# The last layers' first product: two side-by-side 64-row matmuls become two full 128-row ones

## The chip, the cores and the metric

The kernel runs on one NeuronCore of a Trainium2 chip. The metric is device time in microseconds (us) of one execution, as the median of several runs. Beside the times there is one profiled execution of each kernel, from which all rows below come. TensorE multiplies matrices from SBUF into PSUM banks, VectorE, ScalarE and GpSimd do elementwise work, and SyncE issues the DMAs.

## The reference, cut to what matters

A recurrence over 768 steps for 4 batches of 8 heads gives 3072 tokens of 320 values. Two pairs of layers follow. The change lies in the last pair, `_moe2_ref`:

```python
x = _moe_ref(x=x, **moe_kwargs)            # 3072 x 320
h = x @ w_in                               # w_in: 320 x 2048
g = np.maximum(h, 0.0) + alpha * np.minimum(h, 0.0)
return (g @ w_out).astype(np.float32)      # w_out: 2048 x 320
```

## The kernel before

The recurrence runs in 24 slots of chunks (phase 1). Between its products stand those of the first pair of layers. Phase 2 does the rest: the first pair's last tokens, and the whole second pair.

Numbers are float32 held as two parts, a high one that TensorE takes as it is and a low one, the rest. A product of x and w is done as high times high, high times low and low times high. In the second pair the first product contracts 320 inputs, as two row tiles of 128 and one of 64, transposed so that inputs lie on the rows and tokens in the columns. `x2_d[w]` in DRAM holds a window of 256 tokens as five tiles: the high and low part of rows 0 to 127, those of rows 128 to 255, and a fifth tile with the high part of the last 64 inputs in rows 0 to 63 and their low part in rows 64 to 127. The weights' third row tile holds its 64 inputs twice (`_layout` stacks `n[256:]` on itself), so one 128-row matmul with the high weights (`wh[2]` by `x[4]`) covers high times high and high times low for the last inputs. What is left of them is the low weights by the high inputs.

The hidden units are 16 tiles of 128 (`K2`). `mm3` does the first product for one or two of them into PSUM tiles `ph`; the moving rows are the tokens, 256 or 512 columns. Seven matmuls of 128 rows each (line 1016), then one of 64 rows (line 1019). For the first tile of a pair that last one uses rows 0 to 63 of the low weights and of `x[4]`; for the second it uses rows 64 to 127 of the weights and a sixth tile `x[5]`, into which `load_x` (line 1005) loads the high part once more at rows 64 to 127. The two therefore stand in different halves of the array. Then VectorE applies the slope in two steps (`leaky`, lines 595 and 596), ScalarE makes the high part `gh` (line 1025) and GpSimd the low part `gll` (line 1026).

`mm4` does the second product: for each 128 tokens three matmuls of 320 columns into an accumulator `acc` (lines 1037 to 1039). `step` calls `mm3` for the new tiles and then `mm4` for tiles that are older by `LAG`, 2: while VectorE, ScalarE and GpSimd work on a pair, TensorE does the second product of the pair before.

The windows come in groups. The first, `G0`, is window 0 alone, 256 columns, one hidden tile at a time; its 16 steps are threaded by the string `TAIL` between the first pair's last tokens: "s" is a step of `G0`, "a" a first product of the first pair (line 575), "n" its scaling by ScalarE (line 592), "t" and "u" its transposes (line 614), "b" its second product, "o" the transposes out, "w" a load of weights. Then five groups of two windows (512 columns) and one of one window (256 columns) take two tiles a step. The order of TensorE's instructions is the order in which the code is written; the other engines' orders come from a scheduler.

Of the kernel before, what the change touches and what calls it, by code (L numbers as in the profile page):

```python
# [48 lines left out]
def tile_kernel(ctx: ExitStack, tc: tile.TileContext, w_fm, a0_fm, a_fm, kb_fm, r_fm, v_fm, v_tm,  # L49
# [59 lines left out]
    KBP = [ca.tile([128, 1280], F32, name=f"KBS{i}") for i in range(3)]  # L109
    KBS = [t.rearrange("p (e s d) -> p e s d", e=2, d=D) for t in KBP]  # odd heads before even ones  # L110
    XP = ca.tile([128, 320], F32, name="XP")
# [46 lines left out]

# [1 line left out]
    queue, now, seen = [], [0.0], []  # L160
# [28 lines left out]
    def pace(dt, n):  # L189
        """follows dt us in which the array counts n columns: keeps those of the last SPAN us above the floor"""  # L190
        note(dt, n)
        floor, extra = LEVELS[min(st["slot"] // 4, 1) if st["slot"] != 4 else 2] if st["slot"] < NG - 4 else LEVELS[3]
        if more() and counted(dt + 0.09) + n < floor:
            note(0.09, 0)
            while more() and counted() < floor + extra:
                pop()

    def idle(dt):
        """dt us in which the next products wait for other engines"""
        while dt > 0.1 and more():  # L200
            dt -= pop()
        note(max(dt, 0.0), 0)
# [4 lines left out]

# [1 line left out]
    def keep(n):  # L209
# [6 lines left out]

# [1 line left out]
    def prep_load(w):  # L218
# [23 lines left out]
    def check(w, pe):  # L242
        """counts what is out of range"""
        if pe == 0:
            st[w]["H"] = b4.tile([104, 16, 65], F32, name="H")
        wv = st[w]["wt"][pe][:, 0:520].rearrange("p (s k) -> p s k", k=65)[:, :, 1:65]
        for i, sc in ((0, 1.0), (1, -1.0)):
            j = 4 * w + 2 * pe + i
            o = (m1.tile([104, 8, 64], F32, name="over", tag="raw2") if w < 2 else
                 st[w]["H"][:, pe * 8:pe * 8 + 8, 1:65])  # L250
            nc.scalar.activation(out=o, in_=wv, func=AF.Relu, scale=sc, bias=lims[:, i:i + 1],
                                 accum_out=flags[:, j:j + 1])
# [88 lines left out]

# [1 line left out]
    def inverse(W):  # L343
# [62 lines left out]

# [1 line left out]
    def load_g(g):  # L408
# [40 lines left out]
    def blank(p):  # L449
        """zeros in the rows between those of the two heads"""  # L450
        nc.tensor.matmul(p[32:64].rearrange("p s t -> p (s t)"), lhsT=D1[:, 1:17].bitcast(BF16),
                         rhs=D1[:, 0:16 * p.shape[1]].bitcast(BF16), start=True, stop=True)
        note(0.02, 100)
# [96 lines left out]

# [1 line left out]
    def x_move(w):  # L552
# [9 lines left out]

# [1 line left out]
    def mm1(t, piece):  # L564
# [85 lines left out]

# [1 line left out]
    def decode(raw, e, m, o, scales=()):  # L652
        """scales: of column ranges, a factor for each row"""
        v = raw.rearrange("p (n two) -> p n two", two=2)
        low, high = v[:, :, 0], v[:, :, 1].bitcast(I32)
        nc.vector.tensor_scalar(out=e, in0=high, scalar1=0x7FF00000, scalar2=None, op0=ALU.bitwise_and)
        nc.vector.tensor_scalar(out=m, in0=high, scalar1=0xFFFFF, scalar2=None, op0=ALU.bitwise_and)
        nc.scalar.activation(out=e, in_=e, func=AF.Relu, scale=8.0, bias=ebias[0:e.shape[0]])
        nc.scalar.activation(out=f32(m), in_=m, func=AF.Copy, scale=2.0 ** -20, bias=1.0)
        nc.vector.scalar_tensor_tensor(out=e, in0=high, scalar=-0x80000000, in1=e, op0=ALU.bitwise_and,  # L660
                                       op1=ALU.bitwise_or)
        nc.vector.scalar_tensor_tensor(out=f32(m), in0=low, scalar=2.0 ** -52, in1=f32(m), op0=ALU.mult, op1=ALU.add)
        for a, z, sc in scales:
            nc.vector.tensor_scalar(out=f32(m[:, a:z]), in0=f32(m[:, a:z]), scalar1=sc, scalar2=None, op0=ALU.mult)
        nc.gpsimd.tensor_tensor(out=o, in0=f32(m), in1=f32(e), op=ALU.mult)

# [1 line left out]
    def words(src, scales=()):  # L668
        """words of 256 columns a row, or of 512 while the layers' tiles are free, decoded"""
        n = src.shape[1] * src.shape[2]  # L670
        if n > 256:
            st["wide"] = i = 1 - st.get("wide", 0)
            raw = m1.tile([128, 1024], U32, name="raw", tag=("lnh", "P")[i])[:, 0:2 * n]
            em = m1.tile([128, 2, 512], I32, name="wem", tag="lnl")[:, :, 0:n]
            o = raw[:, 0:n].bitcast(F32)
        else:
            raw = m1.tile([128, 512], U32, name="raw2")
            em = m1.tile([128, 2, 256], I32, name="em2")
            o = m1.tile([128, 256], F32, name="dec")
        nc.sync.dma_start(out=raw.rearrange("p (k n) -> p k n", k=src.shape[1]), in_=src.bitcast(U32))  # L680
        decode(raw, em[:, 0], em[:, 1], o, scales)
        return o
# [26 lines left out]
    def cuts(n, wide):  # L709
        """column ranges of 512 or 256"""  # L710
        return [(i, min(i + 512, n)) for i in range(0, n, 512)] if wide else [(i, i + 256) for i in range(0, n, 256)]

# [1 line left out]
    def w2_tasks():  # L714
# [10 lines left out]

# [1 line left out]
    def vec_tasks(w):  # L727
# [25 lines left out]
    def fill_tasks(g):  # L753
        """of the chunk's slot: products that later windows need, by their places in it, and what they wait for"""
        W, c4 = divmod(g, 4)
# [67 lines left out]
    def tail_tasks(g):  # L823
        """of the tokens after the last chunk: transposes in, first products, second ones, transposes out"""
        t1, t2 = g - 3, g - 4
# [128 lines left out]

# [1 line left out]
    KI, KO = 768, 2 * DM  # L956
# [13 lines left out]
    def early_w():  # L970
        """the first weights, where the chunks' preparation was"""
        k = [b2.tile([128, KI + 2 * KO], F32R, name="kbf") for _ in range(2)]
# [9 lines left out]
    def phase2(p2):  # L982
# [12 lines left out]
        def parts(f):  # L995
            """of the weights of 128 hidden units: the three row tiles in, and the rows out"""
            j, q = divmod(f, 2)
            return [([a[:, k * 256 + q * 128:k * 256 + q * 128 + 128] for k in range(3)], b[:, q * DM:q * DM + DM])
                    for a, b in st["w2", j]]

        def load_x(ws, t):
            for i, w in enumerate(ws):
                c = slice(i * 256, i * 256 + 256)
                nc.sync.dma_start(out=f32(t[:, 0:5, c]), in_=f32(x2_d[w][:]))
                nc.sync.dma_start(out=f32(t[64:128, 5, c]), in_=f32(x2_d[w][0:64, 4]))
            return {"x": [t[:, i, 0:256 * len(ws)] for i in range(6)], "n": 256 * len(ws), "ws": ws, "g": {}}

        def mm3(G, fs, sp):
            x, n = G["x"], G["n"]
            ph = [ps_p[i % len(ps_p)].tile([128, 512], F32, name="ph")[:, 0:n] for i in range(len(fs))]  # L1010
            for p, f in zip(ph, fs):
                (wh, _), (wl, _) = parts(f)
                ops = [(wh[0], x[0]), (wh[0], x[1]), (wl[0], x[0]), (wh[1], x[2]), (wh[1], x[3]),
                       (wl[1], x[2]), (wh[2], x[4])]
                for j, (l, r) in enumerate(ops):
                    nc.tensor.matmul(p, lhsT=l, rhs=r, start=j == 0, stop=False)  # L1016
            for i, (p, f) in enumerate(zip(ph, fs)):
                r = slice(64 * i, 64 * i + 64)
                nc.tensor.matmul(p, lhsT=parts(f)[1][0][2][r], rhs=x[4 + i][r], start=False, stop=True)  # L1019
            for p, f in zip(ph, fs):  # L1020
# [28 lines left out]
        def limits():  # L1049
            """whether a decay is out of range"""  # L1050
            nc.vector.tensor_reduce(out=s1, in_=flags, axis=mybir.AxisListType.X, op=ALU.add)
# [13 lines left out]
        def x_tile(i):  # L1065
            return cm.tile([128, 6, 512], F32R, name=("w1h", "w1l")[i % 2])

# [38 lines left out]

# [1 line left out]
    def slow(gs, ps_w):  # L1108
# [244 lines left out]
```

## Time and profile before

| | |
|---|---|
| median of 3 runs | 1180.27 us (1178.73 to 1182.65) |
| span of the profiled execution | 1174.9 us |
| time of the profiled execution around its span | not on the page; the median lies 5.4 us above the span |
| TensorE busy | 994.3 us, 85% of the span |
| VectorE, ScalarE, GpSimd busy | 68%, 44%, 43% |
| mean granted clock of TensorE | 0.896 |

The span goes from the first to the last instruction. Each row of the section on rows is one answer of the trace: a sum over a stretch, a piece of the chain of work that ended last (followed back from the last instruction, so that each piece begins where what it waited for ended), or a line of the timeline with start, duration and what stands on the engine. In the timeline xN merges N instructions of one kind that follow each other, and a duration reaches from the first start to the last end; consecutive matmuls overlap, so starts tell the pace better than durations. The columns after a matmul are the rows and columns of its weights and the shape of its moving rows. Stretches of phase 2 are told by their times: the first group lies between 769.7 and 834.8 us, the five groups of 512 columns between 834.8 and about 1130.6, the last group behind them.

### The profile page before, as it was taken

The numbers are of one execution on the slowest core, as the hardware profiler recorded it, in microseconds if no ns is written. First come the engines' busy times: TensorE is split into PE (matmuls) and PEld (weight loads), VectorE is DVE, ScalarE is ACT, GpSimd is POOL, SyncE is SP. The second block draws the span as 40 slices with busy tenths as digits, with TensorE's granted clock in tenths as the row PEclk, the third lists the DMA queues.
The fourth block names the chain that finished last, engine by engine and source line by source line (L and its number), as shares of the span: only waits on it lengthen the run. The fifth ranks groups of instructions, "written<-read, shape, count | busy, mean of one in ns | idle before, by whom it ended". The sixth has DMA issues, their size and how long they took to land.

```text
span 1174.9 us, 37092 instructions
## 1 busy us (share of the span) xinstructions
PE 994.3 (85%) x15913; PEld 802.3 (68%) x15934; DVE 794.3 (68%) x1610; ACT 516.9 (44%) x1198; POOL 503.1 (43%) x546
## 2 busy tenths in 40 slices
PE   6275686588878978797779878999999999999997
PEld 3233454467666767676667666788888888888886
DVE  8899689978988798879878966556333333333332
ACT  3324454476547663666465647655212121212121
POOL 6848565444434433443444326245233333333332
PEclk8676877789888987888889889999999999999999
DMA  5513344434333433343334333445202020201000
GB/s 167 140 43 94 82 145 123 105 108 126 86 93 107 125 78 93 107 125 78 96 89 119 106 90 94 119 144 169 55 1 73 1 73 1 72 1 48 1 23 15
DMA packets 105423, 100.24 MB, mean 85 GB/s; under 512 B 38244, under 2 KB 84644, under 8 KB 105252
## 3 DMA queue, kind: packets, MB, share of 16 engines
q1 hardware_dynamic: 105252, 97.80, 30.1%
q8 instruction: 127, 2.08, 0.8%
q14 instruction: 44, 0.36, 0.1%
HBM read 72.34 MB, written 25.43 MB: 83 GB/s over the span
## 4 chain that ended last, share of the span: by engine, by line
PE 44%; DVE 32%; ACT 6%; issue 6%; POOL 5%; DMA 5%; SPq 0%; POOLq 0%; DVEq 0%; ACTq 0%
PE ph L1016 13%; PE acc L1037 5%; DVE tmp L354 5%; PE acc L1039 5%; PE acc L1038 5%; DVE LMN L358 4%; PE h L575 4%; DMA kbf<-in_kb_fm_dram 3%; DVE VUS L482 2%; DVE KBS L508 2%; PE ph L1019 2%; DVE XS L336 2%; DVE H L277 2%; DVE P L582 1%; PE pf L465 1%
## 5 line engine op out<-in xcount | busy, mean ns | idle before, releaser
L1026 POOL TENSOR_TENSOR gll<-gt,gh 128x512 fp32r<-128x512 f32 (+1 forms) x112 | 127.1, 1153 | 239.0 <-ACT gh L1025 219.8
L595 DVE TENSOR_SCALAR gt<-ph,al 128x512 f32<-128x512 f32 (+1 forms) x112 | 71.1, 670 | 219.5 <-PE ph L1019 218.0
L1025 ACT CAST gh<-gt 128x512 fp32r<-128x512 f32 (+1 forms) x112 | 61.1, 560 | 268.9 <-DVE gt L596 268.6
L575 PE MATMUL h<-w1h,xt 128*128 128x512 f32 x240 | 104.4, 483 | 16.3 <-ACT h L584 16.3
L312 POOL TENSOR_TENSOR XS<-XS,H 40x512 f32<-40x512 f32 (+1 forms) x48 | 64.9, 1356 | 89.6 <-DVE H L277 53.7
L354 DVE TENSOR_TENSOR tmp<-LMN,LMN 128x87 f32<-128x87 f32 (+25 forms) x189 | 93.5, 506 | 3.4
L1037 PE MATMUL acc<-w2h,gh 128*128 128x320 f32 x288 | 94.0, 326 | 0.0
L1039 PE MATMUL acc<-w2h,gll 128*128 128x320 f32 x288 | 89.1, 309 | 0.3 <-POOL gll L1026 0.3
L1038 PE MATMUL acc<-w2l,gh 128*128 128x320 f32 x288 | 88.9, 309 | 0.0
L211 PE MATMUL busy<-busy 128*128 128x512 bf16 x200 | 61.8, 463 | 28.1 <-DVE tmp L354 22.9
L528 POOL TENSOR_TENSOR YS<-YS,mask 64x512 f32<-64x512 f32 x48 | 64.3, 1339 | 47.6 <-ACT YS L527 42.9
L358 DVE TENSOR_TENSOR LMN<-LMN,tmp 128x87 f32<-128x87 f32 (+25 forms) x189 | 77.1, 419 | 2.7
L575 PEld LDWEIGHTS h<-w1h,xt 128*128 128x128 f32 x240 | 50.0, 219 | 25.8 <-ACT h L584 18.5
L575 PE MATMUL h<-w1l,xt 128*128 128x512 f32 x144 | 67.5, 469 | 0.0
L628 PE MATMUL po<-wo1h,lnh 128*128 128x320 f32 x192 | 66.7, 348 | 0.5 <-DVE lnl L620 0.5
L596 DVE SCALAR_TENSOR_TENSOR gt<-ph,gt 128x512 f32<-128x512 f32 (+1 forms) x112 | 63.9, 606 | 0.5
L630 PE MATMUL po<-wo1h,lnl 128*128 128x320 f32 x192 | 61.5, 320 | 0.2 <-DVE lnl L620 0.2
L629 PE MATMUL po<-wo1l,lnh 128*128 128x320 f32 x192 | 61.5, 320 | 0.0
L211 PEld LDWEIGHTS <-busy 128*128 128x128 bf16 x221 | 23.2, 114 | 55.0 <-DVE busy L945 22.6
L1037 PEld LDWEIGHTS acc<-w2h,gh 128*128 128x128 f32 x288 | 54.1, 188 | 9.6 <-issue 7.4
L581 ACT ACTIVATE P<-h,sm 128x1024 f32<-128x1024 f32 x24 | 26.7, 1114 | 69.0 <-DVE sm L580 65.8
L1016 PE MATMUL ph<-w1h,w2h 128*128 128x512 f32 x180 | 56.6, 396 | 0.0
(214 smaller groups left out, 2718.9 us busy)
## 6 DMA issues: line engine op xcount, KB each, us to landing
kbf<-in_kb_fm_dram SPq DMA_DIRECT2D x24, 416.0 KB
x2d<-x SPq DMA_DIRECT2D x24, 320.0 KB
xd<-Y SPq DMA_DIRECT2D x24, 256.0 KB
xt<-xd SPq DMA_DIRECT2D x12, 512.0 KB
raw<-in_w_in_dram SPq DMA_DIRECT2D x20, 256.0 KB
wt<-in_w_fm_dram SPq DMA_DIRECT2D x24, 211.7 KB
raw<-in_w_in_dram SPq DMA_DIRECT2D x8, 512.0 KB
raw<-in_w_out_dram SPq DMA_DIRECT2D x16, 256.0 KB
```

What stands on the lines that cost most here:

```text
L211: nc.tensor.matmul(st["busy"], lhsT=busy[:, 0:128], rhs=busy, start=True, stop=True)
L312: (nc.vector if w < 2 and e in DA else nc.gpsimd).tensor_tensor(out=o, in0=o, in1=h, op=ALU.mult)
L354: eng.tensor_tensor(out=tv[:, a - rows[0][0]:b - rows[0][0]], in0=M[:, a:b, s:s + 1].to_broadcast(sh), in1=l.unsqueeze(1).to_broadcast(sh) ...
L358: r = eng.tensor_tensor(out=o, in0=o, in1=tv[:, a - rows[0][0]:b - rows[0][0]], op=ALU.add)
L575: nc.tensor.matmul(st["h"][:, ns], lhsT=l, rhs=r, start=j == 0, stop=j == len(ops) - 1)
L595: nc.vector.tensor_scalar(out=tmp, in0=h, scalar1=0.0, scalar2=al, op0=ALU.min, op1=ALU.mult)
L628: nc.tensor.matmul(po, lhsT=lh[:, k], rhs=wo1h[:, k], start=k == 0, stop=False)
L1016: nc.tensor.matmul(p, lhsT=l, rhs=r, start=j == 0, stop=False)
L1026: nc.gpsimd.tensor_tensor(out=gll, in0=t, in1=f32(gh), op=ALU.subtract)
L1037: nc.tensor.matmul(acc, lhsT=gh[:, cs], rhs=oh, start=f == 0, stop=False)
L1038: nc.tensor.matmul(acc, lhsT=gh[:, cs], rhs=ol, start=False, stop=False)
L1039: nc.tensor.matmul(acc, lhsT=gll[:, cs], rhs=oh, start=False, stop=f == K2 - 1)
```

## The change

The low weights of the last inputs are multiplied by the whole of `x[4]`, as an eighth matmul of 128 rows in each tile's own list. As the weights' third tile holds the 64 inputs twice, rows 64 to 127 add low weights times low inputs, a product that was left out before. The second loop goes, and with it the tile `x[5]` and its load. (Comments and doc strings are also removed, by which the lines of `mm3` and `mm4` have numbers lower by 1 to 4.)

```diff
             for i, w in enumerate(ws):
                 c = slice(i * 256, i * 256 + 256)
                 nc.sync.dma_start(out=f32(t[:, 0:5, c]), in_=f32(x2_d[w][:]))
-                nc.sync.dma_start(out=f32(t[64:128, 5, c]), in_=f32(x2_d[w][0:64, 4]))
-            return {"x": [t[:, i, 0:256 * len(ws)] for i in range(6)], "n": 256 * len(ws), "ws": ws, "g": {}}
+            return {"x": [t[:, i, 0:256 * len(ws)] for i in range(5)], "n": 256 * len(ws), "ws": ws, "g": {}}
...
                 ops = [(wh[0], x[0]), (wh[0], x[1]), (wl[0], x[0]), (wh[1], x[2]), (wh[1], x[3]),
-                       (wl[1], x[2]), (wh[2], x[4])]
+                       (wl[1], x[2]), (wh[2], x[4]), (wl[2], x[4])]
                 for j, (l, r) in enumerate(ops):
-                    nc.tensor.matmul(p, lhsT=l, rhs=r, start=j == 0, stop=False)
-            for i, (p, f) in enumerate(zip(ph, fs)):
-                r = slice(64 * i, 64 * i + 64)
-                nc.tensor.matmul(p, lhsT=parts(f)[1][0][2][r], rhs=x[4 + i][r], start=False, stop=True)
+                    nc.tensor.matmul(p, lhsT=l, rhs=r, start=j == 0, stop=j == len(ops) - 1)
...
-            return cm.tile([128, 6, 512], F32R, name=("w1h", "w1l")[i % 2])
+            return cm.tile([128, 5, 512], F32R, name=("w1h", "w1l")[i % 2])
```

TensorE's order at a pair of 512 columns, before, from the pair's first matmul to its first second-product matmuls (`w1h` is here the tile that holds the inputs, `w2h` and `w2l` the high and low weights; the last number of a name tells buffers apart):

```order
L1016 MATMUL ph<-w1h,w2h_11903 128x512 x2
L1016 MATMUL ph<-w1h,w2l_11904 128x512
L1016 MATMUL ph<-w1h,w2h_11903 128x512 x2
L1016 MATMUL ph<-w1h,w2l_11904 128x512
L1016 MATMUL ph<-w1h,w2h_11903 128x512 x3
L1016 MATMUL ph<-w1h,w2l_11904 128x512
L1016 MATMUL ph<-w1h,w2h_11903 128x512 x2
L1016 MATMUL ph<-w1h,w2l_11904 128x512
L1016 MATMUL ph<-w1h,w2h_11903 128x512
L1019 MATMUL ph<-w1h,w2l_11904 128x512 x2
L1037 MATMUL acc_12732<-w2h_11901,gh_12781 128x320
L1038 MATMUL acc_12732<-w2l_11902,gh_12781 128x320
```

The same pair on TensorE now (line 1015 is 1016 of before, 1033 is 1037):

```order
L1015 MATMUL ph<-w1h,w2l_11904 128x512
L1015 MATMUL ph<-w1h,w2h_11903 128x512 x2
L1015 MATMUL ph<-w1h,w2l_11904 128x512
L1015 MATMUL ph<-w1h,w2h_11903 128x512
L1015 MATMUL ph<-w1h,w2l_11904 128x512
L1015 MATMUL ph<-w1h,w2h_11903 128x512 x2
L1015 MATMUL ph<-w1h,w2l_11904 128x512
L1015 MATMUL ph<-w1h,w2h_11903 128x512 x2
L1015 MATMUL ph<-w1h,w2l_11904 128x512
L1015 MATMUL ph<-w1h,w2h_11903 128x512
L1015 MATMUL ph<-w1h,w2l_11904 128x512
L1033 MATMUL acc_12728<-w2h_11901,gh_12777 128x320
```

The two matmuls of line 1019 are gone from the pair's end. Each tile ends with one more matmul of the low weights, the first tile's in the middle of the pair, the second's right before the second product.

VectorE's order over the second and third pair of the first group of 512 columns, before (`gt` is the result for one hidden tile):

```order
L595 TENSOR_SCALAR gt_12718<-ph,al 128x512
L595 TENSOR_SCALAR gt_12725<-ph,al 128x512
L596 SCALAR_TENSOR_TENSOR gt_12718<-ph,gt_12718 128x512
L596 SCALAR_TENSOR_TENSOR gt_12725<-ph,gt_12725 128x512
L595 TENSOR_SCALAR gt_12778<-ph,al 128x512
```

And now:

```order
L595 TENSOR_SCALAR gt_12714<-ph,al 128x512
L596 SCALAR_TENSOR_TENSOR gt_12714<-ph,gt_12714 128x512
L595 TENSOR_SCALAR gt_12721<-ph,al 128x512
L596 SCALAR_TENSOR_TENSOR gt_12721<-ph,gt_12721 128x512
L595 TENSOR_SCALAR gt_12774<-ph,al 128x512
```

Both steps of the pair's first tile now stand before those of its second. SyncE's queue has the same order without the eleven loads of line 1005.

## Rows read from the trace of the kernel before

**Rows 1.** Sums by stretch: us, busy and instructions of PE, PEld, DVE, ACT, POOL; clock, DMA.

```profile
769.70:806.20 36.50, 35.62 (x219) 31.16 (x217) 23.32 (x45) 22.98 (x41) 20.27 (x18) 1.00 0.50 162
806.20:834.80 28.60, 28.58 (x184) 26.00 (x185) 14.31 (x30) 10.71 (x23) 7.40 (x11) 1.00 0.44 125
834.80:1130.60 295.80, 295.66 (x1593) 248.80 (x1590) 104.88 (x162) 55.18 (x101) 100.94 (x80) 1.00 0.10 29
```

**Rows 2.** Chain of waits through one pair of 512 columns: start, us, what.

```profile
997.02 3.27 PE ph L1016 x14
1000.29 0.43 PE ph L1019 x2
1000.73 0.35 PE acc L1037
1001.08 0.15 PE acc L1038
...
1004.30 0.15 PE acc L1039
1004.45 0.23 PE ph L1016
```

**Rows 3.** Timeline of PE at that pair's end: start, us, instruction, times.

```profile
999.90 0.40 PE L1016 MATMUL ph<-w1h,w2h 128*128 128x512 f32 x1
1000.22 0.51 PE L1019 MATMUL ph<-w1h,w2l 64*128 64x512 f32 x2
1000.66 0.42 PE L1037 MATMUL acc<-w2h,gh 128*128 128x320 f32 x1
1000.91 0.31 PE L1038 MATMUL acc<-w2l,gh 128*128 128x320 f32 x1
```

**Rows 4.** Chain of waits through a pair of 256 columns, last group.

```profile
1156.34 1.67 PE ph L1016 x14
1158.01 0.31 PE ph L1019
1158.32 0.34 PE acc L1037
```

**Rows 5.** Chain of waits through a single step of 256 columns, first group.

```profile
821.47 0.83 PE ph L1016 x7
822.30 0.31 PE ph L1019
822.61 0.34 PE acc L1037
```

**Rows 6.** Timeline of PE, from one full product to the next.

```profile
812.80 0.40 PE L575 MATMUL h<-w1l,xt 128*128 128x512 f32 x1
813.04 0.40 PE L1016 MATMUL ph<-XS,w2h 128*128 128x256 f32 x2
```

**Rows 7.** Timeline of PE, then of ACT, in the first group; in brackets idle time before.

```profile
775.19 0.42 PE L1039 MATMUL acc<-kbf,gll 128*128 128x320 f32 x1 [0.36 <-POOL gll L1026]
...
788.25 0.61 PE L614 MATMUL ptr<-ident,P 128*128 128x128 f32 x4
...
806.22 0.66 PE L614 MATMUL ptr<-ident,P 128*128 128x128 f32 x4 [0.54 <-ACT P L592]
...
786.92 1.24 ACT L592 ACTIVATE P<-P,sm 128x1024 f32<-128x1024 f32 x1 [0.56 <-POOL sm L589]
```

**Rows 8.** Line 1016: what its engine waited for, us, times.

```profile
  DVE gt L596: 0.4, 1
```

**Rows 9.** Timeline of PE, the last matmuls.

```profile
1163.91 0.31 PE L1039 MATMUL acc<-w2h,gll 128*128 128x320 f32 x1
...
1164.96 0.41 PE L1039 MATMUL acc<-w2h,gll 128*128 128x320 f32 x1 [0.25 <-POOL gll L1026]
...
1166.38 0.31 PE L1039 MATMUL acc<-w2h,gll 128*128 128x320 f32 x1
```

**Rows 10.** Timeline of POOL in the pair of rows 2.

```profile
1003.65 2.55 POOL L1026 TENSOR_TENSOR gll<-gt,gh 128x512 fp32r<-128x512 f32 x2 [4.88 <-ACT gh L1025]
```

## The prediction, made before the changed kernel ran

> **What bounds the kernel now.** I read the busy sums by stretch first, to find which engine fills the part that the change touches. That part begins with the first line-1016 matmul at 769.7 us. From there TensorE is busy without a break: 35.62 of 36.50 us, then 28.58 of 28.60, then 295.66 of 295.80 [rows 1]. In the longest of these stretches VectorE, ScalarE and GpSimd have 104.88, 55.18 and 100.94 us of work, so about two thirds of their time is free. The granted clock is 1.00 throughout, the 2.4 GHz level, and TensorE does not pause there, so I expect no change of clock. A full TensorE row alone doesn't say that the matmuls stream at their best, since ends are modelled; so I read the chain of waits next. In the long stretch it holds TensorE alone [rows 2]. A pair of hidden tiles takes 1004.45 - 997.02 = 7.43 us, and the 64-row matmuls and what follows them stand in it with more time than their columns. Last I read the timeline for the starts at that place [rows 3].
>
> In rows 2 fourteen full matmuls of 512 columns take 3.27 us, 0.2336 us each; a matmul of 320 columns takes 0.147 us (the 0.15 and 0.14 of the chain, 24 of them in 3.5 us). The two 64-row matmuls then take 0.43 us together and the first matmul after them 0.35. The timeline shows why: the last full matmul starts at 999.90, the 64-row pair 0.32 us later, the next full one 0.44 us after that, and its successor only 0.25 us later instead of 0.147 [rows 3]. The two 64-row matmuls do run together (one row, x2, 0.51 us in all), but getting into them and out of them leaves the array unfed, twice per pair.
>
> **The change part by part.** Each hidden tile has 8 matmuls in the first product as before; the number of TensorE instructions does not change. What changes is that the eighth has 128 rows, follows its own tile's seven, and runs alone.
>
> Pairs of 512 columns. Five groups of two windows, eight pairs each: 40. Before: 3.27 + 0.43 + 0.35 = 4.05 us from the first matmul to the end of the first second-product matmul [rows 2]. After: sixteen steps of 0.2336 and one of 0.147, 3.738 + 0.147 = 3.885. Saved 0.165, times 40: 6.6 us.
>
> Pairs of 256 columns. The last group has one window, eight pairs. Before 1.67 + 0.31 + 0.34 = 2.32 [rows 4]; a step is 1.67 / 14 = 0.119; after 16 x 0.119 + 0.147 = 2.05. Saved 0.265, times 8: 2.1 us.
>
> Singles of 256 columns. The first group handles one tile at a time, so before there was one 64-row matmul with nothing beside it: 0.83 + 0.31 + 0.34 = 1.48 [rows 5]. After 8 x 0.119 + 0.147 = 1.10. Saved 0.38 each; there are 16. Seven come after 806.22; TensorE is busy for 28.58 of the 28.60 us there [rows 1], and all seven count: 2.7 us.
>
> The other nine meet three places where TensorE waits, or would. Three are issued before 775.19, where it waits 0.36 us for GpSimd; two more before the transposes at 788.25, whose input ScalarE finishes at 786.92 + 1.24 = 788.16, only 0.09 us ahead; and three lie between the last product that feeds the transposes of 806.22 and those transposes, which wait 0.54 us for ScalarE [rows 7]. A gain ahead of such a place is taken back there, unless what is waited for comes earlier too. That leaves one single in full, 0.4 us; I take 0.5 with a little for GpSimd's result. The bounds are 0 and 9 x 0.38 = 3.4.
>
> Two places outside these patterns. In the first pair of 512 columns there are only two ph buffers, and the third tile waits for VectorE: 0.4 us once [rows 8]. With the first tile complete eight matmuls earlier most of it goes: 0.3 us. At the end the last two tiles' second product waits for gll: the twelve matmuls from 1163.91 to 1166.38 take 2.47 us where 12 x 0.147 = 1.76 would do [rows 9]. The even tile will be complete eight steps, 0.95 us, earlier, which is more than the 0.71 lost: 0.7 us.
>
> What costs nothing. Eleven small loads leave SyncE's queue; the chain of the long stretch has no DMA in it [rows 2], so they bring nothing either. VectorE, ScalarE and GpSimd do the same instructions, VectorE from the second pair of 512 on in the order of tiles. The even tile's VectorE work now falls beside the next eight matmuls, and the odd tile's beside GpSimd's subtraction. A pair's two subtractions take 2.55 us, from 1003.65 to 1006.20 [rows 10]. If they took twice that, they would end at about 1008.8; in the new order they start nearly 2 us earlier, and their odd tile is first read some 1.8 us after 1008.0, so TensorE covers it. If that cover failed it would cost the excess in each of 48 pairs, 1 us being 48. No stall takes its place that I can see: the next in line is TensorE's own columns.
>
> The price that the trace of before doesn't show is a step from a full ph matmul straight to the first acc matmul. The nearest rows are two full products that follow each other, 812.80 to 813.04, 0.24 us after a matmul of 512 columns [rows 6], and acc to ph, 0.15 us at 1004.30 [rows 2]: both no more than the columns. The far bound is today's 0.35 us instead of 0.147 [rows 2], as if the refill belonged to the end of a product. I take the near value, since those rows have the same change of output and differ only in that no 64-row matmul lies between. On the other side nothing is in sight: a column costs 0.46 ns both at 512 (0.2336 us) and at 320 (0.147 us) [rows 2], so the added steps will not be shorter than the others.
>
> The two sides of this have each a rule in the Trainium skill. The trace shows the two 64-row matmuls starting together [rows 3]. The page "TensorE: Matmul & The Clock Gate", section "Part 3: Packing small matmuls — row/col tiling", says that matmuls in different row groups run at the same time; taken alone it makes the pair one slot, and the time that of the second rival below. The trace also shows 0.32 us into and 0.44 us out of that slot [rows 3]. "TensorEngine Tiling (Array Packing)", section "Key Properties", says that a change of tiling mode drains the engine; by it the excess goes with the 64-row form, as in my sum. The trace agrees with both, and the excess is the larger.
>
> Sum: 6.6 + 2.1 + 2.7 + 0.5 + 0.3 + 0.7 = 12.9 us. The profiled execution's span is 1174.9 us, which becomes 1162.0. The page gives no time around it; the median of the runs, 1180.27, lies 5.4 us above the span, and nothing before 769.7 us or after the last matmul is touched, so I keep the 5.4: 1167.4 us.
>
> **Rivals.**
> *The first group gives nothing.* Its singles are threaded between chains of the three other engines, and 806.22 and 788.16 show how little slack some have [rows 7]. If all of it is taken back, 6.6 + 2.1 + 0.3 + 0.7 = 9.7 remain: 1170.6. Against it: after 806.22 TensorE waits for nothing [rows 1].
>
> *The excess stays, the second slot is added.* Here what starves the array belongs to closing one product and opening the other. The excess of a 512 pair is 4.05 - (15 x 0.2336 + 0.147) = 0.40 us. If it stays, each 512 pair gains a slot of 0.2336 and each 256 pair one of 0.119: 9.3 + 1.0 = 10.3 us, 1190.6, slower. It decides from the point where more than 0.2336 / 0.40, 58%, of the excess stays. For it: no row of before has ph followed by acc without a 64-row matmul. Against it: rows 6, and that 0.32 us pass before the 64-row matmul, ahead of any acc.
>
> *Only the refill stays*, 0.35 in place of 0.147 after each ph product. Pairs of 512 then take 3.738 + 0.35 = 4.09, 0.04 more, 1.5 us in all; those of 256 give 0.07 x 8 = 0.6, seven singles and one 0.19 each, 1.5, and the ends 1.0: 1.6 us saved, 1178.7, no change. For and against as above.
>
> *All nine early singles count*, because the chains they wait on start from TensorE too: 3.4 in place of 0.5, 1164.5.
>
> **How the numbers follow.** Forecast 72%, first group lost 13%, all singles 6%, refill stays 5%, excess stays 4%. Less than 0.3%, 3.5 us, can't be told from no change; so faster by more gets the first, second and third, 91%, same 5%, slower 4%. The range runs from 1163.0, the third case less 1.5 us, to 1172.5, the lost first group with 2 us more, both for the spread of the runs (1178.73 to 1182.65). It leaves out about one in ten, the last two cases and a little.
>
> **What would show it.** In the long stretch the chain should have sixteen ph matmuls and then acc matmuls of 0.15 us at once, a pair 7.26 us apart instead of 7.43; the last group's pairs 3.66 us; singles 0.38 us shorter. The one wait for VectorE [rows 8] and that for gll at the end [rows 9] should go; the wait of the transposes at 806.22 should stay and grow. A first acc matmul of 0.35 us would show the refill rival; GpSimd named as releaser between pairs would make my cover wrong. A pair of 7.4 us or more makes the prediction wrong.

## The result and the profile after

| | before | changed | ratio, 95% interval |
|---|---|---|---|
| median of the first 4 runs each | 1179.87 us | 1167.67 us (1158.72 to 1170.57) | 0.9884 (0.9851 to 0.9917) |
| five further rounds, 11 and 7 runs | 1178.51 us | 1168.74 us | 0.9912 (0.9882 to 0.9942) |
| span of the profiled execution | 1174.9 us | 1164.6 us | |

Both intervals lie wholly below 1: the changed kernel takes about 1% less. (The ratios are those on record; the quotients of the medians, 0.990 and 0.992, lie inside the intervals.) The forecast was 1167.4 us. The profiled execution of the changed kernel took 1166.42 us, 1.8 more than its span.

The runs of one kernel scatter by 10 to 16 us (1173.26 to 1183.74 us before, 1158.72 to 1174.92 changed, in the runs of this table), and the starts of four matmuls say where. In each profile I read the first ph matmul, the first of 512 columns, the first of the last group, and the last matmul of all. Up to the first of these all kernels of this study have the same instructions in the same order.

| kernel | first ph | first group | 512 columns | last group | all behind first ph |
|---|---|---|---|---|---|
| before | 769.73 | 65.09 | 295.86 | 35.70 | 396.65 |
| changed | 773.36 | 61.75 | 288.68 | 32.87 | 383.30 |
| changed, profiled again (e9) | 781.47 | 61.74 | 288.71 | 32.87 | 383.31 |
| 64 rows first (e1) | 776.82 | 65.19 | 295.28 | 34.81 | 395.28 |
| both in one half (e2) | 774.25 | 65.05 | 304.34 | 36.51 | 405.91 |
| each in its own list (e3) | 767.92 | 65.08 | 319.86 | 38.94 | 423.87 |
| 64 rows twice (e4) | 773.15 | 65.89 | 304.81 | 36.65 | 407.35 |
| singles only (e5) | 779.51 | 61.75 | 295.87 | 35.70 | 393.31 |
| pairs only (e6) | 779.34 | 65.07 | 288.68 | 32.87 | 386.62 |
| seven matmuls (e7) | 774.77 | 61.18 | 269.76 | 30.91 | 361.85 |
| eighth at the pair's end (e8) | 776.50 | 61.77 | 289.06 | 33.67 | 384.51 |
| singles moved (e10) | 776.56 | 65.08 | 288.68 | 32.87 | 386.63 |
| one load held back (e11) | 776.16 | 60.52 | 288.71 | 32.87 | 382.09 |

All numbers are us; each stretch is the difference of two starts. What precedes the first ph matmul takes 767.92 to 781.47 us; where a version leaves the later instructions as they were, these repeat to a few hundredths. e1 to e8 ran once each, so their stretches and chains are read and not their times. So the effect is read from the last column: 396.65 - 383.30 = 13.35 us. In the two profiles of the table's first lines the part ahead happened to be 3.6 us longer in the changed kernel, and what follows the last matmul 0.6 shorter, which is why the spans differ by only 10.3.

The sums by stretch of the changed kernel answer to [rows 1] (length, then busy time of TensorE, weight loads, VectorE, ScalarE and GpSimd, clock, DMA share, GB/s):

```profile
773.30:809.20 35.90, 32.78 (x219) 30.16 (x217) 23.29 (x45) 22.82 (x41) 20.46 (x19) 1.00 0.50 165
809.20:835.10 25.90, 25.88 (x184) 25.17 (x185) 13.91 (x30) 10.63 (x23) 7.35 (x11) 1.00 0.40 128
835.10:1123.70 288.60, 288.60 (x1592) 259.33 (x1590) 116.00 (x163) 57.71 (x101) 103.91 (x81) 1.00 0.10 28
```

TensorE is as full as before in the second and third stretch, both are shorter, and the clock is 1.00 as before. In the first it now lacks 3.1 us, where it lacked 0.88. The chain of waits through a pair of 512 columns answers to [rows 2]:

```profile
1000.43 3.73 PE ph L1015 x16
1004.16 0.15 PE acc L1033
...
1007.69 0.46 PE ph L1015 x2
```

Sixteen ph matmuls in 3.73 us, then 0.15 us for the first acc matmul as for every other; the pair has 1007.69 - 1000.43 = 7.26 us instead of 7.43. The timeline at the pair's end, as in [rows 3]:

```profile
1003.77 0.39 PE L1015 MATMUL ph<-w1h,w2l 128*128 128x512 f32 x1
1004.00 0.31 PE L1033 MATMUL acc<-w2h,gh 128*128 128x320 f32 x1
1004.15 0.31 PE L1034 MATMUL acc<-w2l,gh 128*128 128x320 f32 x1
```

From the last ph matmul to acc 0.23 us and from there 0.15, where there were 0.32, 0.44 and 0.25. The chain through a single step and through the last group's pairs, as in [rows 5] and [rows 4]:

```profile
821.15 0.94 PE ph L1015 x8
822.10 0.15 PE acc L1033
```

```profile
1144.19 1.91 PE ph L1015 x16
...
1147.87 1.91 PE ph L1015 x16
```

A single takes 0.94 + 0.15 = 1.09 us to the end of its first acc matmul, before 1.48; a pair of the last group 3.68 instead of 3.94.

What waits in the first group, on TensorE, answers to [rows 7]:

```profile
776.57 0.98 PE L1015 MATMUL ph<-XS,LMN 128*128 128x256 f32 x6 [0.60 <-DVE gt L596]
...
778.80 0.41 PE L1035 MATMUL acc<-kbf,gll 128*128 128x320 f32 x1 [0.73 <-POOL gll L1022]
...
791.64 0.66 PE L614 MATMUL ptr<-ident,P 128*128 128x128 f32 x4 [0.36 <-ACT P L592]
...
805.84 0.55 PE L642 MATMUL ptx<-ident,xs 128*128 128x128 f32 x3 [0.44 <-ACT xs L633]
...
809.22 0.66 PE L614 MATMUL ptr<-ident,P 128*128 128x128 f32 x4 [1.00 <-ACT P L592]
```

The wait for gll has grown from 0.36 to 0.73, that at the last of these transposes from 0.54 to 1.00, and three have come up that were not there: for VectorE at the third single, at the middle transposes, and for the copy that feeds the transposes out. The end, as in [rows 9]:

```profile
1154.90 0.31 PE L1035 MATMUL acc<-w2h,gll 128*128 128x320 f32 x1
...
1155.34 0.31 PE L1035 MATMUL acc<-w2h,gll 128*128 128x320 f32 x1
...
1156.66 0.30 PE L1035 MATMUL acc<-w2h,gll 128*128 128x320 f32 x1
```

The last twelve steps, from 1154.90 to 1156.66, take 1.76 us where they took 2.47; the wait for gll is gone. So is the one for VectorE [rows 8]: the first pair of 512 columns takes 5.57 us instead of 6.04. GpSimd in the pair shown above, as in [rows 10]:

```profile
1004.69 1.30 POOL L1022 TENSOR_TENSOR gll<-gt,gh 128x512 fp32r<-128x512 f32 x1 [4.10 <-ACT gh L1021]
1006.56 1.29 POOL L1022 TENSOR_TENSOR gll<-gt,gh 128x512 fp32r<-128x512 f32 x1 [0.57 <-ACT gh L1021]
```

1.30 and 1.29 us each, half of the 2.55 of before: beside VectorE's work for the odd tile (lines 595 and 596, 1004.27 to 1005.75) it is no slower, and it starts as each tile is complete.

### The profile page after: what moved, and what is told of

The parts are those of the page before. It is cut to its first block, busy times and chain, and to the rows that moved or that the text cites. A ratio compares the mean times of both kernels' runs of the same rounds, so it can differ in the third digit from the quotient of the medians.

```text
span 1164.6 us, 37097 instructions
## 1 busy us (share of the span) xinstructions
PE 978.9 (84%) x15934; PEld 808.5 (69%) x15934; DVE 811.2 (70%) x1610; ACT 520.4 (45%) x1198; POOL 503.7 (43%) x546
## 4 chain that ended last, share of the span: by engine, by line
PE 47%; DVE 29%; POOL 7%; issue 6%; ACT 5%; DMA 5%; SPq 0%; POOLq 0%; DVEq 0%; ACTq 0%
PE ph L1015 15%; DVE tmp L354 5%; PE h L575 5%; PE acc L1035 5%; PE acc L1033 5%; PE acc L1034 5%; DVE LMN L358 4%; DMA kbf<-in_kb_fm_dram 4%; DVE VUS L482 2%; DVE KBS L508 2%; PE pf L465 2%; POOL XS L312 2%; DVE H L277 2%; PE po L628 1%; PE pu L442 1%
## 5 line engine op out<-in xcount | busy, mean ns | idle before, releaser
L595 DVE TENSOR_SCALAR gt<-ph,al 128x512 f32<-128x512 f32 (+1 forms) x112 | 75.4, 673 | 189.8 <-PE ph L1015 189.6
L1033 PE MATMUL acc<-w2h,gh 128*128 128x320 f32 x288 | 89.0, 309 | 0.0
L211 PE MATMUL busy<-busy 128*128 128x512 bf16 x221 | 66.4, 455 | 19.5 <-DVE busy L945 18.2
L596 DVE SCALAR_TENSOR_TENSOR gt<-ph,gt 128x512 f32<-128x512 f32 (+1 forms) x112 | 68.8, 615 | 3.7
L1015 PE MATMUL ph<-w1h,w2h 128*128 128x512 f32 x180 | 59.3, 394 | 0.0
L326 PE MATMUL pg<-XS,kbf 104*32 104x64 f32 x1536 | 38.5, 239 | 22.0 <-DVE kbf L303 12.8
```

Of the source, the lines that this page charges most:

```text
L211: nc.tensor.matmul(st["busy"], lhsT=busy[:, 0:128], rhs=busy, start=True, stop=True)
L595: nc.vector.tensor_scalar(out=tmp, in0=h, scalar1=0.0, scalar2=al, op0=ALU.min, op1=ALU.mult)
L1015: nc.tensor.matmul(p, lhsT=l, rhs=r, start=j == 0, stop=j == len(ops) - 1)
L1033: nc.tensor.matmul(acc, lhsT=gh[:, cs], rhs=oh, start=f == 0, stop=False)
```

## The experiments

The theory, A: what the 64-row matmuls cost is the change from 128 rows to 64 and back, wherever it stands, while side by side they are one slot. The rivals: B, the cost belongs to closing one product and opening another; C, each 64-row matmul pays for itself.

**e1, the 64-row matmuls at the pair's start** (edit of the kernel before):

```diff
+            for i, (p, f) in enumerate(zip(ph, fs)):
+                r = slice(64 * i, 64 * i + 64)
+                nc.tensor.matmul(p, lhsT=parts(f)[1][0][2][r], rhs=x[4 + i][r], start=True, stop=False)
             for p, f in zip(ph, fs):
...
-                    nc.tensor.matmul(p, lhsT=l, rhs=r, start=j == 0, stop=False)
+                    nc.tensor.matmul(p, lhsT=l, rhs=r, start=False, stop=j == 6)
-            for i, (p, f) in enumerate(zip(ph, fs)):
...
```

> The kernel before, with the 64-row matmuls moved from the end of a pair's first product to its start: the second product (acc) then meets only full matmuls on one side and the 64-row pair on the other. Theory A (the cost belongs to changing from 128 rows to 64 and back, wherever that is): pairs of 512 columns stay 7.43 us apart, within 0.05; the excess now stands between acc and ph. Theory B (the cost belongs to the 64-row matmuls being the last before another product, that is to the closing of ph): going from full ph matmuls to acc costs nothing now, and the pair shrinks to 7.0 to 7.2 us. Times of the whole kernel are not told apart by 0.3%; the pair's distance is read from the chain.

The chain through a pair (L1013 is the 64-row line, L1019 the full one):

```profile
1003.68 0.43 PE ph L1013
1004.12 3.46 PE ph L1019 x14
1007.57 0.15 PE acc L1037
...
1011.10 0.42 PE ph L1013
```

7.42 us a pair. The 0.43 us stand before the fourteen now, and these take 3.46 instead of 3.27: the 0.19 that were on the first acc matmul are on the first full ph matmul. From ph to acc it costs nothing, as in the changed kernel. B falls. (In all, e1 is 1.37 us shorter than before: its first pair takes 5.65 us instead of 6.04, and the last group loses 0.89 with the wait for gll, since here too the first tile is complete earlier; see e8.)

**e2, both in one half:**

```diff
-                r = slice(64 * i, 64 * i + 64)
-                nc.tensor.matmul(p, lhsT=parts(f)[1][0][2][r], rhs=x[4 + i][r], start=False, stop=True)
+                r = slice(0, 64)
+                nc.tensor.matmul(p, lhsT=parts(f)[1][0][2][r], rhs=x[4][r], start=False, stop=True)
```

> The kernel before, with both 64-row matmuls of a pair in rows 0 to 63 (the same weights' half and the same input tile for both), so that they can't run side by side; there is still one change into 64 rows and one out of it. Theory A: one slot more, 7.43 + 0.23 = 7.66 us a pair. Theory C (each 64-row matmul pays for itself, because its weights are not loaded ahead): 7.43 + 0.43 = 7.86 or more. If the two did not really overlap in the kernel before: 7.43.

```profile
1006.08 3.26 PE ph L1016 x14
1009.34 0.66 PE ph L1019 x2
1010.00 0.34 PE acc L1037
```

0.66 in place of 0.43, the first acc matmul unchanged, 7.64 us a pair in the median: one slot more, as A has it. The second 64-row matmul costs its columns only, so C falls, and the two did share a slot in the kernel before.

**e3, each in its own tile's list:**

```diff
                 for j, (l, r) in enumerate(ops):
                     nc.tensor.matmul(p, lhsT=l, rhs=r, start=j == 0, stop=False)
-            for i, (p, f) in enumerate(zip(ph, fs)):
-                r = slice(64 * i, 64 * i + 64)
-                nc.tensor.matmul(p, lhsT=parts(f)[1][0][2][r], rhs=x[4 + i][r], start=False, stop=True)
+                nc.tensor.matmul(p, lhsT=wl[2][0:64], rhs=x[4][0:64], start=False, stop=True)
```

> The kernel before, with each tile's 64-row matmul right after that tile's seven full ones, in rows 0 to 63, so that a pair changes into 64 rows twice. Theory A: sixteen slots and two visits of 0.40 us of excess, 7.25 + 0.80 = 8.05 us a pair. Theory B: only the second tile's stands before another product that is not ph; one excess, 7.65. The whole kernel: about 40 x 0.6 = 25 us longer than before under A, 9 under B.

```profile
1000.18 1.62 PE ph L1016 x7
1001.80 0.43 PE ph L1017
1002.23 1.83 PE ph L1016 x7
1004.06 0.43 PE ph L1017
1004.49 0.34 PE acc L1035
```

8.03 us a pair in the median (8.05 under A, 7.65 under B). Each visit takes 0.43 us where a full matmul has 0.23, and the full matmul behind it 0.20 more, whether that is of ph (1.83 for seven instead of 1.62) or of acc (0.34).

**e4, the side-by-side pair twice:**

```diff
-            for i, (p, f) in enumerate(zip(ph, fs)):
-                r = slice(64 * i, 64 * i + 64)
-                nc.tensor.matmul(p, lhsT=parts(f)[1][0][2][r], rhs=x[4 + i][r], start=False, stop=True)
+            for k in range(2):
+                for i, (p, f) in enumerate(zip(ph, fs)):
+                    r = slice(64 * i, 64 * i + 64)
+                    nc.tensor.matmul(p, lhsT=parts(f)[1][0][2][r], rhs=x[4 + i][r], start=False, stop=k == 1)
```

> The kernel before, with the two side-by-side 64-row matmuls issued twice in a row (the last inputs' low weights count double). Theory A: one visit, two slots of two matmuls side by side: 7.43 + 0.23 = 7.66 us a pair. Theory C: each matmul or each side-by-side pair pays again: 7.86 or more.

```profile
1006.17 3.26 PE ph L1016 x14
1009.43 0.66 PE ph L1020 x2
1010.09 0.35 PE acc L1038
```

7.65 us a pair: four matmuls in two slots and one visit's excess. Within a visit the two halves work side by side at full pace.

**e5 and e6, the change in one part alone** (`len(fs) == 1` for e5; `len(fs) == 2` for e6, where singles keep line 1019):

```diff
+                if len(fs) == 1:
+                    ops.append((wl[2], x[4]))
...
-            for i, (p, f) in enumerate(zip(ph, fs)):
+            for i, (p, f) in enumerate(zip(ph, fs) if not (len(fs) == 1) else ()):
```

> The change in the first group alone (steps of one tile); the pairs keep their 64-row matmuls side by side. From the first ph matmul to the first of 512 columns: 65.1 us before, 61.8 now (3.3 less, as in the whole change: 0.6 before the transposes that wait for ScalarE, 2.7 after); pairs 7.43 and 3.93 us apart as before, and the wait for gll at the end stays. Rival (the first group's gain comes from elsewhere): 65 us.

> The change in the pairs alone; the first group keeps its 64-row matmul per tile. First group 65.1 us as before; pairs 7.25 and 3.65 us apart, the stretch of 512 columns 288.7 us against 295.9 (7.2 less), the last group with its tail 32.9 against 35.7 (2.8 less). Together with the run on singles it adds up to the whole change's 13.3 us behind the recurrence if the parts are independent.

By the table e5 has the changed kernel's first group (61.75) and before's rest (295.87 and 35.70), e6 the reverse (65.07, 288.68, 32.87). 3.34 and 10.03 us: the parts add up to 13.37, with nothing given back between them.

**e7, no eighth matmul** (the low weights of the last 64 inputs are left out):

```diff
-                       (wl[1], x[2]), (wh[2], x[4]), (wl[2], x[4])]
+                       (wl[1], x[2]), (wh[2], x[4])]
```

> The changed kernel without the eighth matmul (the low weights of the last 64 inputs are left out). It shows what an added full matmul costs: 2 x 0.2336 = 0.47 us a pair of 512, pairs 6.78 us apart; 0.24 a pair of 256, 3.42. If the array were bound by something other than columns (GpSimd's low parts, VectorE), less than that would go, and gll or gt would be named as releasers.

```profile
1003.97 3.26 PE ph L1015 x14
...
1010.75 1.40 PE ph L1015 x6
```

1010.75 - 1003.97 = 6.78 us a pair. An added full matmul costs 0.47 / 2 us, its own columns; nothing else binds the pairs down to there. In the first group, however, the sixteen matmuls less are worth only 0.57 us in place of 16 x 0.119 = 1.9. That is not more waiting: TensorE is idle there for 2.2 us, in the changed kernel for 3.1. What the trace shows instead is a lower clock behind one wait:

```profile
780.22 0.42 PE L1035 MATMUL acc<-kbf,gll 128*128 128x320 f32 x1 [1.53 <-POOL gll L1022]
781.00:783.50 2.50, 2.50 (x10) 2.16 (x10) 0.55 (x1) 0.59 (x1) 0.17 (x1) 0.50 0.23 36
```

TensorE waits 1.53 us for gll (0.73 in the changed kernel), and from 781.0 to 783.5 us the granted clock is 0.50, the level of 1.2 GHz. From the transposes behind that wait to the next second product 5.36 us pass (781.24 to 786.60) instead of 4.11 (779.50 to 783.61), 1.25 us more; what is left of the difference is not taken apart.

**e8, the full eighth matmuls at the pair's end:**

```diff
-                       (wl[1], x[2]), (wh[2], x[4]), (wl[2], x[4])]
+                       (wl[1], x[2]), (wh[2], x[4])]
...
+            for p, f in zip(ph, fs):
+                nc.tensor.matmul(p, lhsT=parts(f)[1][0][2], rhs=x[4], start=False, stop=True)
```

> The changed kernel with both eighth matmuls (full, 128 rows) at the pair's end, where the 64-row ones stood, so that both tiles are complete together as before. The pairs should stay 7.25 and 3.65 us apart: the form, not the place, made the gain. What the earlier completion of the first tile gave goes back: about 0.7 us at the last second products (wait for gll) and 0.3 us at the third tile of 512 columns (wait for VectorE).

```profile
1159.56 0.42 PE L1037 MATMUL acc<-w2h,gll 128*128 128x320 f32 x1 [0.25 <-POOL gll L1024]
```

Pairs stay at 7.25 and 3.67 us. The wait for gll at the end is back, 0.80 us by the table, and 0.38 us return to the stretch of 512 columns. So the first tile's earlier completion is worth these 1.2 us, and the form of the matmul the rest.

**e9, the changed kernel again:**

> The changed kernel once more, unedited, in five rounds against the kernel before. The part up to the first ph matmul has the same instructions in all ten kernels profiled so far and took 767.9 to 779.5 us in them, so the whole time should scatter by several us from run to run; the part behind it should be 383.3 us again, 13.3 less than before's 396.65. Expected ratio about 0.989, with 0.985 to 0.993 open to the scatter. If the gain were an accident of one profile, the part behind would differ from 383.3 by more than 0.3 us.

383.31 us behind the first ph matmul, 0.01 from the first profile, in an execution that was 8.1 us later to get there.

**e10, singles moved ahead of the waits for ScalarE:**

```diff
-TAIL = "... s1 n1 w4 o0 s1 t1 s1 u1 a1 w5 s1 b1 s1 n2 o1 s1 w6 t2 s1 u2 a2 ..."
+TAIL = "... s1 n1 w4 o0 s2 t1 u1 a1 w5 s1 b1 s1 n2 s1 o1 w6 s1 t2 u2 a2 ..."
```

> The changed kernel with three single steps of the first group moved ahead of the places where TensorE waits for ScalarE (the transposes t1 and t2, and the transposes out, o1); the same work in another order. If the gain of the early singles was taken back by those waits (0.67, 0.74 and 1.30 us between starts in the changed kernel's first group), work put into them brings 1 to 2 us of it back: first group 61.75 to about 60.3. Rival (the waits only move on, because their chains start from products that now come later): 61.5 or more. In the whole time it is within the scatter.

It failed: 65.08 us, all of the first group's gain lost. A moved step brings its second product forward too, and that waits, on TensorE:

```profile
811.58 0.50 PE L1015 MATMUL ph<-XS,w2h 128*128 128x256 f32 x2 [0.78 <-DVE gt L596]
...
814.60 0.41 PE L1035 MATMUL acc<-w2h,gll 128*128 128x320 f32 x1 [1.51 <-POOL gll L1022]
...
817.09 0.78 PE L575 MATMUL h<-w1h,xt 128*128 128x512 f32 x1
817.67 0.63 PE L575 MATMUL h<-w1l,xt 128*128 128x512 f32 x1
```

GpSimd hadn't the low parts ready (1.51 us), VectorE not the ph buffer (0.78). The first product that follows then starts at 0.42 to 0.58 us a matmul of 512 columns, where 0.23 is usual. The sums by stretch show the granted clock there:

```profile
810.50:816.40 5.90, 3.10 (x21) 2.34 (x20) 4.17 (x11) 3.72 (x8) 4.48 (x5) 1.00 0.00 0
816.40:820.50 4.10, 4.08 (x13) 3.43 (x14) 1.61 (x3) 1.11 (x3) 0.73 (x1) 0.58 0.28 84
```

TensorE was busy for 3.10 of 5.90 us, and the granted clock in the 4.1 us after that is 0.58 on average, part of it at the lower level of 1.2 GHz. Of the 3.3 us lost, 1.4 are more idle time in the first group (4.57 us against 3.13 in the changed kernel) and about 1.65 lie in that slow part: from those transposes to the next ph matmul 5.76 us pass (816.42 to 822.18) instead of 4.11 (811.54 to 815.65). Other waits took over, as the rival expectation has it; the clock was in neither.

**e11, one load held back.** In the changed kernel GpSimd does the difference of the weights w6 right ahead of the small operation (line 588) that ScalarE's scaling needs, whose own input comes from VectorE (line 587):

```profile
805.74 0.20 DVE L587 TENSOR_SCALAR sm<-sm 128x1 f32<-128x1 f32 x1
804.70 2.41 POOL L967 TENSOR_TENSOR w2l<-w2l,w2h 128x768 fp32r<-128x768 f32 x1
807.07 0.55 POOL L588 TENSOR_TENSOR sm<-sm,half 128x1 f32<-128x1 f32 x1
```

```diff
-                load_w(int(x[1:]))
+                if x == "w6":
+                    with tc.issue_after(st["nrm"].ins):
+                        load_w(6)
+                else:
+                    load_w(int(x[1:]))
```

(`st["nrm"]` is the scaling's instruction, of line 592.)

> The changed kernel with one load of weights (w6: its two roundings on ScalarE, its differences on GpSimd and VectorE) held back until the scaling by ScalarE (line 592) whose result the transposes at 809.22 wait for. In the changed kernel GpSimd's difference of w6, 2.41 us from 804.70, stands ahead of the small operation (line 588) that this scaling needs, and so does some of VectorE's share. If that is what holds the early singles' gain back, the wait at those transposes (1.30 us between starts, 1.15 more than without a wait) shrinks by 1 us or more and the first group falls from 61.75 to 60.0 to 60.8 us. Rival (the wait's chain is bound by ScalarE and VectorE without w6, or another wait takes over as in the reordered run): 61.5 us or more. The rest behind stays 321.55 us; in the whole time it is within the scatter.

GpSimd there now:

```profile
808.59 0.55 POOL L588 TENSOR_TENSOR sm<-sm,half 128x1 f32<-128x1 f32 x1 [1.06 <-DVE sm L587]
809.21 0.19 POOL L589 TENSOR_TENSOR sm<-sm 128x1 f32<-128x1 f32 x1
809.38 1.85 POOL L967 TENSOR_TENSOR w2l<-w2l,w2h 128x768 fp32r<-128x768 f32 x1
```

The first group falls to 60.52 us, 1.23 less, and no wait stands before those transposes any more. Counted from the first ph matmul, line 588 starts 1.28 us earlier (32.43 us instead of 33.71). The input was complete at 805.94 in the changed kernel, so 1.13 us of that were spent behind GpSimd's difference; the edit also moves w6's work on ScalarE and VectorE, and their share is the small rest. This version also took less time than before: 1163.62 us against 1181.24 of before in the same rounds, ratio 0.9868 (0.9816 to 0.9921); against the changed kernel its gain shows in the first group alone, not in the times.

## Why the prediction was right

That the median lies 0.3 us from the forecast is partly luck, since the part ahead of the first ph matmul alone scatters by 13.6; the part behind it is the test: 12.9 us forecast, 13.35 measured.

- Pairs of 512 columns with the wait for VectorE: 6.6 + 0.3 = 6.9 forecast, 295.86 - 288.68 = 7.18 measured. e8 parts it: 295.86 - 289.06 = 6.80 for the form and 0.38 for the wait. The step was right and a little small: the pair's distance fell by 0.177 us in the median, not 0.165.
- Last group with the wait for gll: 2.1 + 0.7 = 2.8 forecast, 2.83 measured, by e8 2.03 for the form and 0.80 for the wait.
- Singles behind the transposes: 2.7 forecast; from their start to the first of 512 columns 834.82 - 806.22 = 28.60 before and 835.11 - 809.22 = 25.90 now, 2.70 less.
- Singles ahead of them: 0.5 forecast, 0.63 measured, out of 9 x 0.38 = 3.4. That they would be taken back was right; by what, only in part. The prediction's "busy without a break" was loose for this stretch: [rows 1] leave 0.88 us idle there, the two waits of [rows 7]. Those two grew and the wait at the middle transposes appeared, as forecast, but I did not foresee those for VectorE at the third single and for the copy before the transposes out. e11 shows one source: the load of w6, above all GpSimd's queue, in which a difference of weights stood ahead of what the scaling needs. With it out of the way 1.2 us of the lost gain come back.
- Cover: no engine took TensorE's place among the pairs (e7 shows that 0.47 us a pair more could go).
- The price that the trace of before did not show, ph straight to acc, was the near bound: 0.23 and 0.15 us. The rival in which the excess stays with the product's end is refuted by the changed kernel and by e1, that in which only the refill stays likewise.
- The two rules of the Trainium skill. "TensorEngine Tiling (Array Packing)", section "Key Properties", has a change of tiling mode drain the engine; the runs agree that the change costs, some 0.40 us a visit (e1, e3), but none shows that it is a drain (see the last section). "TensorE: Matmul & The Clock Gate", section "Part 3: Packing small matmuls — row/col tiling", has matmuls of different row groups run together; the runs agree, two slots for four matmuls (e4) against two slots for two in one half (e2). What decides between them is the ratio of slot to visit.
- The time around the span, which I took as 5.4 us from the median, is 1.8 in the later executions. It did not matter, because the gain was subtracted from the median; it means that the profile of before was of a shorter run than the median.

## What to carry to other kernels

Two half-height matmuls side by side save a slot and pay for the change into and out of that form. Here one visit costs 0.40 us at 512 columns against a slot of 0.2336, so it must carry two slots of side-by-side pairs before it wins, and for one slot full matmuls with a half that isn't needed are cheaper. For two the win is small: e4's pair takes 7.65 us, and with four full matmuls in place of its four 64-row ones it would take 7.25 + 0.47 = 7.72, an estimate from the changed kernel and e7. Read such a cost from the starts around it and not from its duration; and where an early part of a kernel scatters, compare the stretch behind it.

## What the runs showed of the hardware that I had not expected

The visit's excess has two halves that stay the same wherever the visit stands: some 0.20 us on the 64-row slot (0.43 for 0.2336) and 0.19 to 0.20 on the next full matmul, be it in the same product (e1, e3) or another (before, e2, e4). They hardly depend on the columns: at 256 the slot has 0.31 instead of 0.119 us and the next full matmul 0.34 instead of 0.147 [rows 5].

The weight loads, of 0.19 us each, show a place where such a half could come from. Before, at the pair of [rows 3], and in the changed kernel at the same place:

```profile
1000.22 0.19 PEld L1019 LDWEIGHTS ph<-w1h,w2l 64*128 64x128 f32 x2 [0.36 <-issue]
1000.66 0.19 PEld L1037 LDWEIGHTS acc<-w2h,gh 128*128 128x128 f32 x1 [0.25 <-issue]
```

```profile
1003.77 0.19 PEld L1033 LDWEIGHTS acc<-w2h,gh 128*128 128x128 f32 x1
```

In the changed kernel the load for the first acc matmul (1004.00) starts 0.23 us ahead of it. Before, the load of the 64-row matmuls (1000.22) and that of the full matmul behind them (1000.66) start only with their matmuls. Whether a half of the excess is this load, no longer hidden, or an array that first runs empty, no run takes apart.

The lower clock was not expected either. Twice, in e7 and e10, a gain in the first group was lost in part because the granted clock fell after TensorE had waited (1.53 us at one place in e7; 2.8 of 5.9 us in e10).

The stretch up to the first ph matmul, with the same instructions each time, took 767.92 to 781.47 us in thirteen profiles, while the stretches behind it repeat to 0.03 us between the two profiles of the changed kernel. The mean granted clock over that part does not tell the short ones from the long ones: it is 0.84 to 0.86 in all thirteen, 0.85 at 767.92 us, 0.86 at 776.82 and 0.84 at 781.47. The cause of the scatter is open.
